# The first layer of an ELU network on one core: seven block products for the 384-token blocks too

## The chip, the core and the metric

The kernel runs on one core of one Trainium2 chip. The metric is the device time of one execution in microseconds (us). Before the change it is 615.97 us, the median of three runs (615.86 to 616.35). TensorE (PE) multiplies, with a row of its own for weight loads (PEld); VectorE (DVE) and ScalarE (ACT) work element by element, GpSimd (POOL) does one integer addition per weight tile, and SyncE (SP) issues nearly all transfers (DMAs).

## The reference

```python
# q, k, v: (4, 12, 448, 64); cap = 30
scores = cap * tanh(q @ k.T / sqrt(64) / cap)
attn = softmax(scores) @ v
x = attn.transpose(0, 2, 1, 3).reshape(1792, 768)     # tokens x d_model
h = x @ w_in                                           # 768 x 2048
g = where(h > 0, h, exp(min(h, 0)) - 1)
return g @ w_out                                       # 2048 x 768
```

## The kernel before, in words

First the attention (to about 161 us of the span), then the two-layer network, which the change is about. All matrices of the network stand transposed on the chip: 128 rows of d_model or d_ff by tokens. The 1792 tokens are four blocks t = 0 to 3, two of 384 tokens (the small blocks) and two of 512 (the large ones). d_model is six chunks of 128 (c), d_ff 16 tiles of 128, taken in eight rounds r = 0 to 7 of two tiles (`FT`). Every fp32 operand is split into a high and a low part, and a product is three matmuls: high by high, high by low, low by high (`products`, L404). So one chunk of the contraction costs three matmuls of one block's width.

A round has a first layer (`hidden`, L421: six chunks, 18 matmuls for each of two d_ff tiles and each block), the ELU (`exp` on ACT, `bend` on DVE, `high` on ACT, `low` on DVE) and a second layer (`pair`, L460: two output tiles e and e + 1, 12 matmuls together, in one of three rooms of two PSUM banks), whose result DVE adds to the sum over rounds (`gather`, L473).

From round 1 on the large blocks' first layer goes by seven products in place of eight. The pair of blocks by the two halves of d_model, and the two d_ff tiles by the same halves, are 2 by 2 quarters of three chunks each. Sums of x quarters and sums of weight quarters (`sum`, `form_high`, `form_low` of `Weights`, each round anew) are multiplied as blocks 1 to 7 (`block`, L483), nine matmuls each, m1 to m7. Blocks 6, 7, 4 and 5 take sums of x, which are formed once (`combine`, `form_high`, `form_low` of `Tokens`), stored in DRAM (`send`) and fetched every round into a ring of three buffers of one chunk (`fetch`, L288). m1 is copied out of PSUM by ACT (`keep`, c1), m6 is added to c1 (u2), m7 to u2 (u3), m4 to u3 (c), m2 to c1, m3 to u2, m5 to u3 and u2 (`add`, L495, on DVE). c, c1, u3 and u2 are then what `hidden` would have given, in SBUF and not in PSUM.

Blocks and `hidden` share two PSUM banks in turn (`bank`, L416): a block can't begin before the one two places ahead of it has been read out.

Each engine runs its instructions in program order. That order is written by a planner: a step has an engine, a duration, a due time, what it needs, and rooms it takes and frees; `Plan.run` plays the steps through and emits them in that order, the steps of TensorE in the order in which `plan_products` lists them. Weight tiles come through one raw buffer `pre` (`load`), then ACT, DVE and POOL unpack them (`plan_tile`) and DVE makes the weight sums (`plan_forms`). Transfers are steps of an engine d and stand in SP's queue in the order of the plan.

Of the kernel before, what the change touches and what calls it, by code (L numbers as in the profile page):

```python
# [213 lines left out]
class Tokens:  # L214


    def __init__(self, nc, pool, early):
# [32 lines left out]
    def first(self):  # L250
        for c in range(NC):
            self.parts[1, c] = [
                self.next.tile([P, BLOCKS[1][1]], F32R, name=f"x{i}1_{c}", tag=f"x{i}", bufs=NC) for i in "hl"
            ]

    def combine(self, i, k):

        x = [[self.block(HC * j + i, PAIR + n) for n in range(2)] for j in range(2)]
# [15 lines left out]
    def form_high(self, n, i):
        t = self.chunk(n, i)
        self.nc.scalar.activation(out=t[:, 0], in_=self.form(n, i), func=AF.Copy)
        self.ring.setdefault(n, []).append((t[:, 0], t[:, 1]))
        self.whole[n, i] = t

    def form_low(self, n, i):  # L280
        h, l = self.ring[n][i]
        self.nc.vector.tensor_tensor(out=l, in0=self.form(n, i), in1=h.bitcast(F32), op=ALU.subtract)

    def send(self, n, i):
        d = self.forms[n, i] = self.dr.tile([P, 2, BANK], F32, name=f"form{n}_{i}", tag=f"form{n}_{i}", bufs=1)
        self.nc.sync.dma_start(out=d, in_=self.whole.pop((n, i)).bitcast(F32))
# [981 lines left out]
```

## Time and profile before

| | |
|---|---|
| time, median of three runs | 615.97 us |
| time of the profiled execution | 616.79 us |
| its span, first to last instruction | 614.9 us |
| PE busy | 605.9 us, 99% |
| DVE busy | 475.9 us, 77% |
| ACT busy | 365.1 us, 59% |
| DMA, mean over the span | 168 GB/s, 49% of 16 engines |
| granted TensorE clock | 0.998 of full speed |

The 1.9 us between the span and the time lie outside the first and the last instruction. Matmuls overlap in the profile (a matmul of 384 columns is shown as 0.33 to 0.34 us long, while the next one starts about 0.17 us after it), so the pace is read from starts and not from durations. One round of the network is 55.7 us long, from 1 on; the last matmul starts at 608.5 us.

### The profile page before, as it was taken

The page shows a single profiled execution, that of the slowest core. Times are in us where ns is not written, and L with a number is a line of the kernel's source. Part 1 is how long each engine was busy: PE and PEld are TensorE (multiplying, and loading weights), DVE is VectorE, ACT ScalarE, POOL GpSimd, SP SyncE. Part 2 cuts the span into 40 slices and gives each one's busy share as a digit, 9 for nine tenths or more (in the row PEclk, how much of TensorE's full clock was granted, in tenths as well). Part 3 has the DMA queues.
Part 4 walks back from the last instruction along what each step waited for, and adds up shares of the span by engine and source line. Part 5 has one row for each costly group of instructions (what it writes and reads, how often), then busy time and mean ns, then how long its engine had stood idle before and what let it go on. Part 6 is the DMA issues. An engine that isn't in the chain of part 4 may idle for free.

```text
span 614.9 us, 8926 instructions
## 1 busy us (share of the span) xinstructions
PE 605.9 (99%) x3347; PEld 472.0 (77%) x3347; DVE 475.9 (77%) x684; ACT 365.1 (59%) x527; POOL 63.1 (10%) x40
## 2 busy tenths in 40 slices
PE   8999999999999999999999999999999999999996
PEld 3444444444788889888988988898899889888984
DVE  5898999998779966977896687779668857874473
ACT  6999999999876674724545354454445435441330
POOL 0010010010100112112102111211110112110000
PEclk9999999999999999999999999999999999999999
DMA  5456457571221778644535445464444445352444
GB/s 188 162 170 197 142 140 225 154 197 57 88 48 58 281 299 270 221 153 165 192 107 206 155 161 193 157 228 166 172 163 146 155 155 205 136 220 80 163 157 176
DMA packets 39622, 103.08 MB, mean 168 GB/s; under 512 B 11026, under 2 KB 15890, under 8 KB 39570
## 3 DMA queue, kind: packets, MB, share of 16 engines
q1 hardware_dynamic: 39282, 101.90, 48.9%
q8 instruction: 28, 0.46, 0.3%
q10 hardware_dynamic: 288, 0.52, 0.3%
q14 instruction: 24, 0.20, 0.1%
HBM read 90.44 MB, written 11.88 MB: 166 GB/s over the span
## 4 chain that ended last, share of the span: by engine, by line
PE 97%; ACT 1%; DMA 0%; DVE 0%; issue 0%; SPq 0%; ACTq 0%
PE o L408 12%; PE o L407 12%; PE o L406 12%; PE pv L861 10%; PE s L819 8%; PE h L407 6%; PE h L406 6%; PE h L408 6%; PE m L408 6%; PE m L407 6%; PE m L406 6%; PE sum L905 3%; PE pv L874 2%; PE s L836 2%; DMA pre<-in_qk_dram 0%; ACT p L854 0%
## 5 line engine op out<-in xcount | busy, mean ns | idle before, releaser
L408 PE MATMUL o<-gh,wl 128*128 128x384 f32 (+1 forms) x380 | 137.8, 363 | 0.0
L406 PE MATMUL o<-gh,wh 128*128 128x384 f32 (+1 forms) x380 | 137.6, 362 | 0.0
L407 PE MATMUL o<-gl,wh 128*128 128x384 f32 (+1 forms) x380 | 137.5, 362 | 0.0
L476 DVE TENSOR_TENSOR x<-o,x 128x768 f32<-128x768 f32 (+1 forms) x83 | 90.0, 1086 | 24.7 <-PE o L408 24.3
L148 POOL TENSOR_TENSOR wv<-wv,wq 128x768 int32<-128x768 int32 x24 | 46.7, 1946 | 370.0 <-DVE wv L145 354.6
L852 ACT ACTIVATE s<-s 128x896 f32<-128x896 f32 x84 | 76.6, 912 | 4.7 <-PE s L836 3.6
L854 ACT ACTIVATE p<-s 128x896 f32<-128x896 f32 x84 | 77.1, 918 | 2.7
L407 PEld LDWEIGHTS o<-gl,wh 128*128 128x128 f32 x380 | 71.4, 188 | 7.7
L408 PEld LDWEIGHTS o<-gh,wl 128*128 128x128 f32 x380 | 71.3, 188 | 7.7 <-DVE wl L159 0.2
L406 PEld LDWEIGHTS o<-gh,wh 128*128 128x128 f32 x380 | 71.4, 188 | 7.6
L407 PE MATMUL h<-xl,wh 128*128 128x384 f32 (+1 forms) x210 | 71.5, 340 | 0.0
L406 PE MATMUL h<-xh,wh 128*128 128x384 f32 (+1 forms) x210 | 71.5, 340 | 0.0
L408 PE MATMUL h<-xh,wl 128*128 128x384 f32 (+1 forms) x210 | 71.3, 339 | 0.0
L861 PE MATMUL pv<-p,vf 128*64 128x448 f32 x276 | 59.5, 552 | 0.0
L449 ACT ACTIVATE gh<-e 128x384 fp32r<-128x384 f32 (+1 forms) x64 | 36.7, 574 | 26.8 <-DVE e L439 26.6
L439 DVE SCALAR_TENSOR_TENSOR e<-e,h 128x384 f32<-128x384 f32 (+1 forms) x36 | 20.2, 564 | 33.1 <-ACT e L435 33.1
L453 DVE TENSOR_TENSOR gl<-e,gh 128x384 fp32r<-128x384 f32 (+1 forms) x64 | 40.0, 630 | 5.9 <-ACT gh L449 5.8
L406 PEld LDWEIGHTS h<-xh,wh 128*128 128x128 f32 x210 | 39.4, 188 | 3.0 <-DVE e L439 0.7
L407 PEld LDWEIGHTS h<-xl,wh 128*128 128x128 f32 x210 | 39.4, 188 | 2.1 <-DVE xl L248 0.8
L861 PEld LDWEIGHTS pv<-p,vf 128*64 128x64 f32 x276 | 16.8, 136 | 31.0 <-issue 23.3
L408 PEld LDWEIGHTS h<-xh,wl 128*128 128x128 f32 x210 | 39.4, 188 | 0.6
L434 ACT ACTIVATE e<-h 128x384 f32<-128x384 f32 (+1 forms) x36 | 18.0, 499 | 35.5 <-PE h L408 35.3
(132 smaller groups left out, 1019.2 us busy)
## 6 DMA issues: line engine op xcount, KB each, us to landing
t<-form SPq DMA_DIRECT2D x81, 512.0 KB, 5.5
pre<-in_w_dram SPq DMA_DIRECT2D x32, 768.0 KB, 4.4
raw<-in_qk_dram SPq DMA_DIRECT2D x22, 448.0 KB, 4.5
form<-t SPq DMA_DIRECT2D x12, 512.0 KB, 3.4
vf<-in_v_dram SPq DMA_DIRECT2D x23, 256.0 KB, 4.3
rb<-rec SPq DMA_DIRECT2D x48, 112.0 KB, 2.9
out_dram<-x SPq DMA_DIRECT2D x5, 512.0 KB, 2.8
out_dram<-x SPq DMA_DIRECT2D x6, 384.0 KB, 2.5
```

The source lines that it names most:

```text
L148: nc.gpsimd.tensor_tensor(out=vi, in0=vi, in1=q, op=ALU.add)
L406: mm(acc, wh[:, m, :], ph, start=first, stop=False)
L407: mm(acc, wh[:, m, :], pl, start=False, stop=False)
L408: mm(acc, wl[:, m, :], ph, start=False, stop=last)
L439: self.nc.vector.scalar_tensor_tensor(out=e, in0=e, scalar=-1.0, in1=self.h.pop(k), op0=ALU.add, op1=ALU.max)
L449: self.nc.scalar.activation(out=self.g[k][0], in_=self.e[k], func=AF.Copy)
L453: self.nc.vector.tensor_tensor(out=gl, in0=self.e.pop(k), in1=gh.bitcast(F32), op=ALU.subtract)
L476: self.nc.vector.tensor_tensor(out=o, in0=self.o.pop((r, t, e)), in1=o, op=ALU.add)
L819: yield lambda a=a, b=b, i=i: self.nc.tensor.matmul(s, a[o, k], b[o, :S], start=i == 0, stop=i == 2)
L852: self.nc.scalar.activation(out=s, in_=s, func=AF.Tanh, scale=self.con.tanh_scale)
L854: self.nc.scalar.activation(out=pt, in_=s, func=AF.Exp, scale=self.con.exp_scale)
L861: self.nc.tensor.matmul(out[o, :S], w[j], x[j], **flags)
```

## The change

The small blocks take the seven-product scheme too, from round 2 on (`FROM`); in rounds 0 and 1 they still go by `hidden`. `plan_block` has a second argument h: 1 for the large pair of blocks, 0 for the small. The names now carry it: m6_1_2 is block 6 of the large pair in round 2, m6_0_2 that of the small.

The small blocks' sums need x itself, while `leave` writes the second layer's sum over it; so the first 768 token columns of x are parked in DRAM (`park`, six transfers), taken back in twelve pieces (`unpark`), summed (`combine`, 12 on DVE), split (`form_high`, 12 on ACT, and `form_low`, 12 on DVE) through one of two buffers, and stored (`send`). Sums of both kinds are fetched every round. Three chunks of block 1's split x (c < 3 of t = 1) no longer stay in SBUF: round 1 fetches them (`plan_both`), which pays for two more buffers, "more", so that from round 2's small blocks on five buffers take the fetches in turn.

The order of TensorE's work is now a list for each kind of round (`ORDERS`): a number is a block (1 to 7 of the large pair, 11 to 17 of the small), a pair `(t, i)` a `hidden`, a triple `(back, t, e)` one output pair of the second layer of the round `back` rounds ago. Due times have changed too (`DUES`, `ELU`, `ADD`, `GATHER`, `LEAD`).

```diff
-NEXT = {6: (3, 0), 7: (4, 0), 4: (1, 0), 5: (2, 1)}
+ORDER = (*range(HC, NC), *range(HC))
+FROM = (2, 1)
+LEAD = 10.1
+DUES = ((-21.5, -17.4, -10.3, 4.0, 13.0), (-19.6, -29.7, -25.7, -5.8, 14.8), (-20.2, -16.9, -7.6, 6.0, 18.4))
...
+    (
+        6, 1, 2, 7, 3, (1, 3, 0), 4, (1, 3, 2), 11, (1, 3, 4), 5, (0, 2, 0), (0, 2, 2), (0, 2, 4), (0, 3, 0),
+        17, (0, 3, 2), (0, 3, 4), 16, 14, 12, 13, 15,
+    ),
...
+    def park(self, c):
+        width = 2 * BLOCKS[0][1]
+        d = self.kept[c] = self.dr.tile([P, width], F32, name=f"park{c}", tag=f"park{c}", bufs=1)
+        self.nc.sync.dma_start(out=d, in_=self.all[:, c, :width])
+
+    def unpark(self, j, k, i):
+        width = BLOCKS[0][1]
+        t = self.raw[j, k, i] = self.half.tile([P, width], F32, name=f"back{j}{k}{i}", tag="back", bufs=4)
+        self.nc.sync.dma_start(out=t, in_=self.kept[HC * j + i][:, k * width : k * width + width])
...
+    def fetch(self, h, r, n, i, room):
         if i == 0:
-            self.ring[n] = []
-        t = self.chunk(f"{r}_{n}", i)
-        self.nc.sync.dma_start(out=t.bitcast(F32), in_=self.forms[n, i])
-        self.ring[n].append((t[:, 0], t[:, 1]))
+            self.ring[h, n] = []
+        if room == "ring":
+            t = self.chunk(f"{h}_{r}_{n}_{i}")
+        else:
+            t = self.half.tile([P, 2, BANK], F32R, name=f"t{h}_{r}_{n}_{i}", tag="more", bufs=2)
+        t = t[:, :, : BLOCKS[2 * h][1]]
+        self.nc.sync.dma_start(out=t.bitcast(F32), in_=self.forms[h, n, i])
...
-    def plan_block(self, n, r):
+    def plan_block(self, n, h, r):
         p, x, wt = self.plan, self.x, self.wt
+        t, width = 2 * h, BLOCKS[2 * h][1]
...
+    def plan_fetches(self):
+
+        steps, turn = [], 0
+        for due, h, r, b, i in self.uses:
+            if (h, r, b) == (1, 1, 2):
+                continue
+            room = "ring"
+            if (r, h) >= (FROM[0], 0) and (r, h) != (FROM[0], 1):
+                room, turn = ("ring", "ring", "ring", "more", "more")[turn], (turn + 1) % 5
...
+        for r, order in enumerate(ORDERS[:3] + ORDERS[3:4] * (NR - 4) + ORDERS[4:]):
             self.begun[r] = self.clock
...
+            for k in order:
+                if isinstance(k, int):
+                    self.plan_block(k % 10, 1 - k // 10, r)
+                elif len(k) == 1:
+                    self.plan_both(r)
+                elif len(k) == 2:
+                    self.plan_first(r, *k)
+                else:
+                    back, t, e = k
+                    self.plan_second(r - back, t, e)
...
         p.room("ring", HC)
+        p.room("more", 2)
+        p.room("back", 4)
+        p.room("stage", 1)
+        p.room("wq", 1)
         self.plan_products()
+        self.plan_fetches()
         self.plan_opening(normalised)
+        self.plan_smaller(self.begun[FROM[0]])
```

Three places show how instructions move. The first is TensorE at the start of round 2. Before, block 1 (its last row stands here) is followed by block 6, and this by the small blocks' first layer (h4):

```order
L408 MATMUL m1_2_2889<-xh2_2_1945,wl8_2685 128x512
L406 MATMUL m6_2_2901<-t2_2_0_2811,forms_1889 128x512
L407 MATMUL m6_2_2901<-t2_2_0_2811,forms_1889 128x512
L408 MATMUL m6_2_2901<-t2_2_0_2811,forms_1889 128x512
L406 MATMUL m6_2_2901<-t2_2_1_2833,forms_1889 128x512
L407 MATMUL m6_2_2901<-t2_2_1_2833,forms_1889 128x512
L408 MATMUL m6_2_2901<-t2_2_1_2833,forms_1889 128x512
L406 MATMUL m6_2_2901<-t2_2_2_2840,forms_1889 128x512
L407 MATMUL m6_2_2901<-t2_2_2_2840,forms_1889 128x512
L408 MATMUL m6_2_2901<-t2_2_2_2840,forms_1889 128x512
L406 MATMUL h4_0_2919<-xh0_0_882,wh8_2684 128x384
```

Now block 6 comes first (its last row stands here), then block 1, and then block 2:

```order
L468 MATMUL m6_1_2_2969<-t1_2_2_2_2928,forms_1883 128x512
L466 MATMUL m1_1_2_2988<-xh2_0_1921,wh8_2785 128x512
L467 MATMUL m1_1_2_2988<-xl2_0_1922,wh8_2785 128x512
L468 MATMUL m1_1_2_2988<-xh2_0_1921,wl8_2786 128x512
L466 MATMUL m1_1_2_2988<-xh2_1_1941,wh8_2785 128x512
L467 MATMUL m1_1_2_2988<-xl2_1_1942,wh8_2785 128x512
L468 MATMUL m1_1_2_2988<-xh2_1_1941,wl8_2786 128x512
L466 MATMUL m1_1_2_2988<-xh2_2_1950,wh8_2785 128x512
L467 MATMUL m1_1_2_2988<-xl2_2_1951,wh8_2785 128x512
L468 MATMUL m1_1_2_2988<-xh2_2_1950,wl8_2786 128x512
L466 MATMUL m2_1_2_3019<-xh2_3_1974,wh8_2785 128x512
```

Block 2, the third in this order, takes the bank that block 6 had; before, the third there was h4, in the bank of block 1. Later in round 2, blocks 6 and 4 of the small pair stand next to each other, behind an output pair and ahead of blocks 2, 3 and 5:

```order
L468 MATMUL o2_3_4_3339<-gh5_3_3249,wl11_3173 128x512
L466 MATMUL m6_0_2_3357<-t0_2_2_0_3261,forms_1883 128x384
L467 MATMUL m6_0_2_3357<-t0_2_2_0_3261,forms_1883 128x384
L468 MATMUL m6_0_2_3357<-t0_2_2_0_3261,forms_1883 128x384
L466 MATMUL m6_0_2_3357<-t0_2_2_1_3279,forms_1883 128x384
L467 MATMUL m6_0_2_3357<-t0_2_2_1_3279,forms_1883 128x384
L468 MATMUL m6_0_2_3357<-t0_2_2_1_3279,forms_1883 128x384
L466 MATMUL m6_0_2_3357<-t0_2_2_2_3315,forms_1883 128x384
L467 MATMUL m6_0_2_3357<-t0_2_2_2_3315,forms_1883 128x384
L468 MATMUL m6_0_2_3357<-t0_2_2_2_3315,forms_1883 128x384
L466 MATMUL m4_0_2_3379<-t0_2_4_0_3331,wh9_2903 128x384
```

The bank of m4_0_2 is the one that block 7 (m7_0_2) had, two output pairs earlier.

The second place is VectorE ahead of the addition of block 6 in round 2. wv are weight tiles that are unpacked, wl and gl low parts, x_123 the sum over rounds, e the ELU. Before, the eleven instructions up to that addition are:

```order
L476 TENSOR_TENSOR x_123<-o1_1_4_2783,x_123 128x2x384
L439 SCALAR_TENSOR_TENSOR e3_3_2842<-e3_3_2842,u3_1_2631 128x512
L439 SCALAR_TENSOR_TENSOR e2_3_2860<-e2_3_2860,u2_1_2553 128x512
L476 TENSOR_TENSOR x_123<-o1_2_0_2818,x_123 128x2x512
L453 TENSOR_TENSOR gl3_3_2882<-e3_3_2842,gh3_3_2881 128x512
L453 TENSOR_TENSOR gl2_3_2886<-e2_3_2860,gh2_3_2885 128x512
L476 TENSOR_TENSOR x_123<-o1_2_2_2846,x_123 128x2x512
L129 TENSOR_SCALAR wv10_2797<-wv10_2797 128x768
L132 TENSOR_SCALAR wv10_2797<-wv10_2797 128x768
L145 SCALAR_TENSOR_TENSOR wv10_2797<-pre_73,wv10_2797 128x768
L501 TENSOR_TENSOR u2_2_2925<-c1_2_2905,m6_2_2901 128x512
```

Now the twelve up to it are these; stage is the low part of a small block's sum of x, and the lines that read pre_73 and wv9 into forms are weight sums:

```order
L338 TENSOR_TENSOR stage2_1_2948<-back111_2793,stage2_1_2948 128x384
L514 TENSOR_TENSOR gl3_3_2954<-e3_3_2897,gh3_3_2953 128x512
L241 TENSOR_TENSOR forms_1883<-pre_73,forms_1883 128x384
L241 TENSOR_TENSOR forms_1883<-wv9_2829,forms_1883 128x384
L241 TENSOR_TENSOR forms_1883<-pre_73,forms_1883 128x384
L241 TENSOR_TENSOR forms_1883<-wv9_2829,forms_1883 128x384
L159 TENSOR_SCALAR wv10_2925<-wv10_2925 128x768
L162 TENSOR_SCALAR wv10_2925<-wv10_2925 128x768
L175 SCALAR_TENSOR_TENSOR wv10_2925<-pre_73,wv10_2925 128x768
L500 SCALAR_TENSOR_TENSOR e2_3_2930<-e2_3_2930,u2_1_1_2567 128x512
L537 TENSOR_TENSOR x_123<-o1_2_0_2882,x_123 128x2x512
L562 TENSOR_TENSOR u2_1_2_3012<-c1_1_2_3006,m6_1_2_2969 128x512
```

From the addition of m4 in round 1 to this addition, the two included, VectorE had 34 instructions before. Now it has 36: 5 additions of a block, 4 sums of x (`combine`), 3 `form_low` of them, 8 instructions that unpack three weight tiles, 4 sums of weight quarters and their 4 low parts, 3 `bend`, 2 `low`, and 3 `gather` (two of 768 columns, one of 1024).

The third place is SP's queue in round 4. pre is a raw weight tile, t a fetched chunk of a sum of x. Before:

```order
L106 DMA pre_73<-in_w_dram 128x1536
L294 DMA t4_3_0_3882<-form3_0_2402 128x1024
L294 DMA t4_3_1_3897<-form3_1_2420 128x1024
L294 DMA t4_3_2_3913<-form3_2_2448 128x1024
L106 DMA pre_73<-in_w_dram 128x1536 x2
L294 DMA t4_4_0_4027<-form4_0_2302 128x1024
L294 DMA t4_4_1_4039<-form4_1_2357 128x1024
L294 DMA t4_4_2_4056<-form4_2_2375 128x1024
L106 DMA pre_73<-in_w_dram 128x1536
L294 DMA t4_1_0_4139<-form1_0_2261 128x1024
L294 DMA t4_1_1_4154<-form1_1_2310 128x1024
L294 DMA t4_1_2_4169<-form1_2_2361 128x1024
```

Now, a piece of the same round, with the small pair's blocks 7 (t0_4_3), 6 (t0_4_2) and 4 (t0_4_4):

```order
L354 DMA t0_4_3_0_4149<-form0_3_0_2690 128x2x384
L354 DMA t0_4_3_1_4160<-form0_3_1_2951 128x2x384
L136 DMA pre_73<-in_w_dram 128x1536
L354 DMA t0_4_3_2_4197<-form0_3_2_3181 128x2x384
L354 DMA t0_4_2_0_4217<-form0_2_0_2709 128x2x384
L354 DMA t0_4_2_1_4222<-form0_2_1_2963 128x2x384
L354 DMA t0_4_2_2_4249<-form0_2_2_3192 128x2x384
L354 DMA t0_4_4_0_4276<-form0_4_0_2810 128x2x384
L354 DMA t0_4_4_1_4282<-form0_4_1_3040 128x2x384
L354 DMA t0_4_4_2_4295<-form0_4_2_3227 128x2x384
```

In between, in both orders, stand the reads of other blocks' chunks that the pieces leave out. Twelve chunks a round were fetched; now it is 24 from round 2 on, between the same four weight tiles, and a fetch waits for the buffer of the fetch five places ahead of it.

## Rows read from the trace of the kernel before

**Rows 1.** The page's first part: busy us, share of the span, instructions.
```profile
PE 605.9 (99%) x3347; PEld 472.0 (77%) x3347; DVE 475.9 (77%) x684; ACT 365.1 (59%) x527; POOL 63.1 (10%) x40
```
**Rows 2.** Waits of PE behind its first instruction: us in total, times, longest.
```profile
PE s L836 <- DMA pre<-in_qk_dram: 0.8, 1, 0.8
PE s L819 <- ACT p L854: 0.7, 1, 0.7
```
**Rows 3.** Busy time of each engine in stretches of one round, 1 to 3.
```profile
core 0: us, PE busy (x) PEld busy (x) DVE busy (x) ACT busy (x) POOL busy (x), PEclk, DMA share, GB/s
208.20:263.90 55.70, 55.70 (x279) 49.97 (x278) 44.41 (x70) 36.94 (x59) 7.54 (x4) 1.00 0.72 257
263.90:319.60 55.70, 55.70 (x280) 50.13 (x279) 43.40 (x62) 25.46 (x41) 7.41 (x4) 1.00 0.49 170
319.60:375.30 55.70, 55.70 (x280) 50.13 (x279) 41.35 (x59) 25.39 (x41) 7.38 (x4) 1.00 0.49 170
```
**Rows 4.** Timeline of PE, round 2: start us, us, instruction; 17, 9, 36 matmuls between.
```profile
279.64 0.39 PE L407 MATMUL o<-gl,wh 128*128 128x512 f32 x1
...
283.49 0.40 PE L406 MATMUL m<-t,forms 128*128 128x512 f32 x1
...
285.59 0.33 PE L406 MATMUL h<-xh,wh 128*128 128x384 f32 x1
...
291.83 0.33 PE L406 MATMUL o<-gh,wh 128*128 128x384 f32 x1
```
**Rows 5.** Groups of VectorE instructions by form: busy us, mean ns, idle before.
```profile
L476 DVE TENSOR_TENSOR x<-o,x 128x1024 f32<-128x1024 f32 x41 | 50.0, 1221 | 17.0 <-PE o L408 16.9
L476 DVE TENSOR_TENSOR x<-o,x 128x768 f32<-128x768 f32 x42 | 40.0, 954 | 7.8 <-PE o L408 7.4
...
L145 DVE SCALAR_TENSOR_TENSOR wv<-pre,wv 128x768 int32<-128x768 int32 x24 | 22.9, 954 | 0.4
L159 DVE TENSOR_TENSOR wl<-wv,wh 128x768 fp32r<-128x768 f32 x24 | 22.9, 954 | 9.2 <-ACT wh L155 9.2
...
L453 DVE TENSOR_TENSOR gl<-e,gh 128x512 fp32r<-128x512 f32 x32 | 21.5, 682 | 0.7 <-ACT gh L449 0.7
...
L439 DVE SCALAR_TENSOR_TENSOR e<-e,h 128x384 f32<-128x384 f32 x32 | 17.6, 550 | 33.1 <-ACT e L435 33.1
...
L132 DVE TENSOR_SCALAR wv<-wv 128x768 int32<-128x768 int32 x24 | 13.4, 557 | 0.5
...
L211 DVE TENSOR_TENSOR forms<-pre,forms 128x384 fp32r<-128x384 f32 x14 | 7.7, 551 | 1.4 <-ACT forms L207 1.4
...
L201 DVE TENSOR_TENSOR pre<-pre 128x384 f32<-128x384 f32 x7 | 3.9, 558 | 0.2
```
**Rows 6.** Timeline at round 2's blocks 1 and 6: their last matmuls, copy, addition.
```profile
266.72 0.39 PE L408 MATMUL m<-xh,wl 128*128 128x512 f32 x1
...
267.15 0.60 ACT L493 ACTIVATE c<-m 128x512 f32<-128x512 f32 x1 [3.48 <-PE m L408]
...
268.82 0.39 PE L408 MATMUL m<-t,forms 128*128 128x512 f32 x1
...
269.32 0.69 DVE L501 TENSOR_TENSOR u<-c,m 128x512 f32<-128x512 f32 x1 [0.80 <-PE m L408]
```
**Rows 7.** Line L294, the fetches: from issue to landing, over 81 fetches.
```profile
DMA to landing us min/median/max: 3.4/5.5/8.3
```
**Rows 8.** Line L439, `bend`: duration ns min/median/max, from PSUM, from SBUF.
```profile
L439 DVE SCALAR_TENSOR_TENSOR e<-e,h x36: 486/554/681, 160.7 to 572.9; 128x384 f32<-128x384 f32 x32, 128x512 f32<-128x512 f32 x4
...
L439 DVE SCALAR_TENSOR_TENSOR e<-e,u x14: 678/683/2243, 261.7 to 596.5; 128x512 f32<-128x512 f32 x14
```
**Rows 9.** DMA in round 1's stretch, 208.2 to 263.9 us: GB/s in 40 slices.
```profile
GB/s 403 412 394 18 338 394 394 179 362 303 294 150 371 124 341 365 315 204 287 172 354 303 318 150 309 229 332 291 300 165 71 247 265 9 59 335 382 324 35 0
```

More of the change, by code (lines that the diff above doesn't have):

```diff
@@ L250, in first @@
     def first(self):
[L251 to L258, printed above, removed]
+        width = BLOCKS[1][1]
+        for c in range(HC, NC):
+            self.parts[1, c] = [self.next.tile([P, width], F32R, name=f"x{i}1_{c}", tag=f"x{i}", bufs=HC) for i in "hl"]
@@ new lines, in second, with part, change @@
+    def second(self):
+        self.half = self.open("half")
+        for c in range(HC):
+            t = self.whole[0, 0, c] = self.half.tile([P, 2, BLOCKS[1][1]], F32R, name=f"x1_{c}", tag="x1", bufs=HC)
+            self.parts[1, c] = [t[:, 0], t[:, 1]]
+    def part(self, r, t, c):
+        return self.ring[0, 0][c] if r and t == 1 and c < HC else self.parts[t, c]
+    def change(self, name):
+        self.shut("half")
+        self.half = self.open(name)
+    def park(self, c):
+        width = 2 * BLOCKS[0][1]
+        d = self.kept[c] = self.dr.tile([P, width], F32, name=f"park{c}", tag=f"park{c}", bufs=1)
+        self.nc.sync.dma_start(out=d, in_=self.all[:, c, :width])
@@ L264, in combine, with chunk, form @@
         )[k]
+        o, a, b = (self.raw[*n, i] if small else self.block(HC * n[0] + i, PAIR + n[1]) for n in (o, a, b))
         self.nc.vector.tensor_tensor(out=o, in0=a, in1=b, op=ALU.subtract)
-    def chunk(self, n, i):
-        return self.back.tile([P, 2, BANK], F32R, name=f"t{n}_{i}", tag="ring", bufs=HC)
-    def form(self, n, i):
+    def chunk(self, n):
+        return self.back.tile([P, 2, BANK], F32R, name=f"t{n}", tag="ring", bufs=HC)
+    def form(self, h, n, i):
         j, k = {1: (0, 0), 3: (0, 1), 2: (1, 1), 4: (1, 0)}[n]
-        return self.block(HC * j + i, PAIR + k)
@@ L274, in form_high @@
[L274 to L286, printed above, removed]
@@ L288, in fetch, with form_high @@
-    def fetch(self, r, n, i):
-        if r >= NR:
-            return
-        if i == 0:
-            self.ring[n] = []
-        t = self.chunk(f"{r}_{n}", i)
-        self.nc.sync.dma_start(out=t.bitcast(F32), in_=self.forms[n, i])
-        self.ring[n].append((t[:, 0], t[:, 1]))
-    def quarter(self, j, k):
-        return [self.parts[PAIR + k, HC * j + i] for i in range(HC)]
+        return self.block(HC * j + i, PAIR + k) if h else self.raw[j, k, i]
+    def form_high(self, h, n, i, other=False):
+        if h:
+            t = self.chunk(f"{n}_{i}")
+            self.ring.setdefault((h, n), []).append((t[:, 0], t[:, 1]))
+        else:
+            pool, tag = (self.weights.pool, "wq") if other else (self.half, "stage")
+            t = pool.tile([P, 2, BLOCKS[0][1]], F32R, name=f"stage{n}_{i}", tag=tag, bufs=1)
+        self.whole[h, n, i] = t
+        self.nc.scalar.activation(out=t[:, 0], in_=self.form(h, n, i), func=AF.Copy)
@@ L301, with quarter @@
+    def quarter(self, h, j, k):
+        return [self.parts[2 * h + k, HC * j + i] for i in range(HC)]
 class Step:
@@ L528, in plan_first @@
         bank = ("h", r, t, i)
-        for c in range(NC):
-            more = {"takes": ("bank", bank)} if c == 0 and (r, t) != (0, 0) else {}
+        for k, c in enumerate(ORDER if t == 1 else range(NC)):
+            more = {"takes": ("bank", bank)} if k == 0 and (r, t) != (0, 0) else {}
             needs = [("w", self.tile(f, 0))] + [("x", t, c)] * (t > 0)
-            if c == NC - 1:
+            if k == NC - 1:
                 more["gives"] = ("p", r, t, i)
@@ L541, in plan_second @@
         needs = [("g", r, t, i) for i in range(FT)] + [("w", self.tile(r * FT + i, 1)) for i in range(FT)]
-        for e in range(0, NC, 2):
+        for e in range(0, NC, 2) if only is None else (only,):
             single = last and e == NC - 2
@@ L652, in plan_tile, with users @@
+    def users(self, r, i):
+        keys = []
+        for h in range(2):
+            if r < FROM[h]:
+                keys += [("p", r, 2 * h + j, i) for j in range(2)]
+            else:
+                keys += [("m", n, h, r) for n in ((1, 2), (4,))[i]]
+        return keys
     def plan_tile(self, k, due):
```

284 lines of the change are left out of this document (178 added, 106 removed), and 3 rows, old and new, of the table ORDERS.

## The prediction

> **What bounds the kernel now.** I read the busy shares first: TensorE (PE) is busy 99% of the span, VectorE (DVE) 77%, ScalarE 59% [rows 1]. Busy can hide waiting, so the waits of PE come next: behind its first instruction no wait is longer than 0.8 us [rows 2]. The stretches of one round then say the same of the part that changes: PE 55.70 of 55.70 us, DVE 41 to 44 us, the DMA engines about half busy, but 0.72 in round 1 [rows 3]. So the time of the network is the number of matmuls by their pace, and whatever takes matmuls away helps as long as PE still never waits.
>
> The pace comes from starts [rows 4]. 36 matmuls of 384 columns on x in SBUF take 291.83 - 285.59 = 6.24 us, 0.1733 us each. 17 of the second layer's 512 columns take 3.85 us, 0.2265 each; 9 of 512 columns on a fetched chunk take 2.10 us, 0.2333 each. The granted clock is 1.00 throughout [rows 3].
>
> **What goes.** In rounds 2 to 7 the small pair has 7 blocks of 9 matmuls in place of 4 `hidden` of 18: 63 for 72, so 54 matmuls of 384 columns less. 54 x 0.1733 = 9.4 us off the path, if nothing else moved.
>
> **What comes, beside other work.**
>
> - DVE gains, in each round from 2 on, seven additions of 384 columns out of PSUM. None stands in the trace; the nearest is the `bend` of 384 columns, which reads PSUM and SBUF too, 0.550 us [rows 5]. 7 x 0.55 = 3.9 us on a round of 41 to 43 [rows 3]: 45 to 47 of a round that is now 55.7 - 1.6 = 54.1 us. It fits, and PE hides it. ScalarE gains one copy a round and has the room (25 us of 55.7).
> - Once, 12 `combine` and 12 `form_low` of 384 columns, the first of them in round 1 and the last in round 2. Like weight sums (0.558) and their low parts (0.551) [rows 5]: 24 x 0.55 = 13.2 us. DVE in rounds 1 and 2 then has 44.4 + 43.4 + 13.2 + 3.9 = 104.9 us in 55.7 + 54.1 = 109.8 us. That is 96%; here PE is no longer a safe cover.
> - SP gains 75 fetches of 0.39 MB (12 a round from 2 on, 3 in round 1). A later round moves 170 GB/s x 55.7 us = 9.5 MB [rows 3], plus 12 x 0.39 = 14.2 MB in 54.1 us, 262 GB/s. Round 1 of before ran at 257 GB/s and PE did not wait there [rows 2, 3], so the later rounds are covered on the mean. Rounds 1 and 2 move 14.3 + 9.5 MB of before, 15 fetches (5.9), 12 stores of small sums (4.7) and 8 `unpark` of 0.2 (1.6): 36 MB in 109.8 us, 328 GB/s. The single slices of round 1 go to 412 [rows 9]. So it fits, with little to spare.
>
> **What comes on the path.** Three waits of PE, all in rounds 1 and 2, and a slower pace.
>
> 1. *Block 2 of the large pair in round 2.* It needs block 6's bank, so the addition of m6 must be over, and this stands behind 35 other DVE instructions, counted from the addition of m4 in round 1. Their sum [rows 5, 6, 8]: 5 additions at 0.69, 3 `bend` at 0.683, 4 `combine` and 3 `form_low` at 0.551, 2 long unpacking ones and 2 low parts of weight tiles at 0.954, 4 short unpacking ones at 0.557, 4 weight sums at 0.558 and 4 low parts at 0.551, 2 low parts of 512 at 0.682, and gathers of 0.954, 0.954 and 1.221. That is 3.45 + 2.05 + 3.86 + 3.82 + 2.23 + 2.23 + 2.20 + 1.36 + 3.13 = 24.3 us. DVE can't begin it before block 4's last matmul plus the 0.50 us between 268.82 and 269.32 [rows 6], so m2 starts 24.8 us after that matmul at the earliest. PE alone would be there after 0.23 + block 3 (9 x 0.2265 = 2.04) + two output pairs of 384 (24 x 0.1733 = 4.16) + block 5 (2.10) + three pairs of 512 (36 x 0.2265 = 8.15) + blocks 6 (2.10) and 1 (2.04) = 20.8 us. PE waits 4.0 us somewhere on this way, block 5's fetch and block 6's weight sums included: whichever is late first, DVE sets the end. Before, 34 instructions of much the same sum lay from the one addition to the other, but PE had block 2 and a third pair of 384 more there (4.1 us), and so 0.80 us of idle time still stood ahead of the last addition [rows 6]. If some of this DVE work overlapped less badly than counted, the floor is the chain in itself: block 1's last matmul, copy by ScalarE (starts 0.43 us later, takes 0.60), addition 0.69: 1.72 - 0.23 = 1.5 us.
> 2. *Block 4 of the small pair in round 2* follows block 6 at once and needs block 7's bank; m7 can be added only to u2, which the addition of m6 makes. 0.50 + 0.55 + 0.55 us after block 6's last matmul, less the 0.17 at which PE would go on: 1.4 us. From round 3 on an output pair (12 matmuls of 512, 2.7 us) or more stands between, and hides it.
> 3. *The third chunk of a block in round 2*, three fetches behind stores and a weight tile. A fetch lands after 3.4 to 8.3 us, 5.5 the median [rows 7]. One chunk late by 0 to 5.5 - 3.4 = 2.1 us; I take 0.4, near zero, since round 1 of before had the same load and no wait.
> 4. *The pace on fetched chunks.* 216 matmuls (4 blocks x 9 x 6 rounds) that read fetched chunks of 384 columns do not stand in the trace. Between 0.1733 and 0.1733 + (0.2333 - 0.2265) = 0.180 us: 0 to 1.5 us in sum; I take half, 0.8.
>
> The waits come to 4.0 + 1.4 + 0.4 + 0.8 = 6.6 us, and the change to -9.4 + 6.6 = -2.8 us. The profiled execution took 616.79 us (614.9 of span and 1.9 around it), so 614.0 by its measure; the median of the runs is 0.8 lower, 615.97 - 2.8 = 613.2 us.
>
> **Rivals.**
>
> *The gain comes through.* DVE's work in the first wait may be lighter than the means make it, and only the two short chains are left: -9.4 + 1.5 + 1.4 = -6.5, 609.5 us. For it: nearly all of that work comes in forms that are in the trace, and a little could be done before block 4. Against: they stand in that order in the program, and no engine overtakes itself.
>
> *A fetch is late in each of the later rounds (slower).* In round 4 the third chunk of block 6 of the small pair gets the buffer of block 7's first chunk. From there to its use PE has two more chunks (6 x 0.1733 = 1.04 us), an output pair of 512 (12 x 0.2265 = 2.72) and two chunks of block 6 (1.04): 4.8 us. A fetch that lands in the median 5.5 us costs 0.7 a round, in 7 us 2.2, in 8.3 us 3.5. Rounds 3 to 6 have this order. At 7 us, 4 x 2.2 = 8.8: 622.0 us; the gain is undone from 0.7 us a round, which is the median. For it: that median. Against: the 3.4 us are a fetch alone, the longer ones had two or three issued at once [rows 7], and this one is alone in SP's queue. The Trainium skill (DMA: Bandwidth & Descriptors, "Where 436 GB/s comes from") says that about 358 GB/s bind between HBM and SBUF; the slices above 358 in round 1 do not agree with it as a hard limit here [rows 9]. By it rounds 1 and 2 would be 328 / 358 = 92% full, and by the highest slice 80%: the first would give this rival twice the chance that the second does.
>
> *VectorE is held up by GpSimd in the later rounds (slower).* In rounds 2 to 7 four `bend` a round go from PSUM and SBUF to two inputs in SBUF. Of this kind one took 2.24 us in place of 0.683; none that reads PSUM was over 0.681 [rows 8]. The small pair's blocks 2, 3 and 4 stand behind each other in rounds 2 to 6, and each bank has 9 x 0.1733 = 1.56 us to come back, of which 0.50 + 0.55 - 0.17 = 0.9 are taken by the addition: 0.7 us of slack. One hold-up of 1.56 us at that place costs 0.9 us, 4.5 us in five rounds: 617.7 us. It undoes the gain from three such hits. For it is the rule in the Trainium skill (SBUF — State Buffer, "Who interferes with whom") that a VectorE instruction with two SBUF inputs contends with a GpSimd one that reads SBUF, and one of the two then blocks fully; the 2.24 us agree. Against: one in 14 was hit, and GpSimd works only 7.4 us of a round [rows 3].
>
> **How the numbers follow.** 0.64 for the forecast, with a range of its own from 611.5 (the third and fourth term zero, half a us less in the first) to 616 (the third and fourth at their upper ends, DVE 1 us late at the start of the first). 0.10 for the full gain, 0.12 for late fetches, 0.14 for GpSimd. The range 610 to 619 leaves out less than two in ten: half of the first rival below, most of the late fetches above. What a measurement of this kernel can tell from no change is about 0.2%, 1.2 us, so faster means under 614.7. The forecast is under it with about 0.8 of its chance (0.51), within it with 0.16 of 0.64 (0.10): faster 0.51 + 0.10 = 0.61; same 0.10 and 0.05 of the two slow rivals in their mild forms, 0.15; slower 0.24.
>
> **What would show it.** Right: 54 matmuls fewer; PE starts 4 us apart in sum between block 5 of round 1 and block 2 of round 2, 1.4 us ahead of the small pair's block 4 in round 2, and none from round 3 on; a later round about 54 us long, with DVE at 46 and the DMA near 262 GB/s; 0.174 to 0.180 us a matmul in the small blocks on fetched chunks. Wrong: gaps of PE that return every round, at a fetched chunk (the second rival) or with a VectorE instruction over 2 us ahead of them (the third); a wait in round 2 under 2 us (the first); or a wait before round 1, where I count none.

## The result and the profile after

The changed kernel takes 625.09 us (median of four runs, 622.63 to 626.76), the kernel before 615.91 beside it: a ratio of 1.0145, 95% interval 1.0108 to 1.0182. It is slower by 9 us, where 2.8 us less were forecast. The profiled execution took 624.2 us and spans 622.4.

The first part of the page (answers to [rows 1]):

```profile
PE 603.7 (97%) x3293; PEld 464.5 (75%) x3293; DVE 516.8 (83%) x750; ACT 370.3 (59%) x545; POOL 64.5 (10%) x40
```

54 matmuls fewer, as counted, but PE no longer fills its span. Its waits from 165 us on (answer to [rows 2]; us in total, times, longest):

```profile
PE m L466 <- DMA t<-form: 4.5, 7, 1.4
PE m L466 <- DVE u L562: 3.1, 2, 1.8
PE h L467 <- DVE xl L278: 2.8, 2, 2.0
```

The windows (columns as in [rows 3]) say where. The first row is the opening of the network, then the end of round 1, the start of round 2, round 3, and a later round:

```profile
165.00:185.00 20.00, 17.22 (x86) 15.45 (x85) 12.91 (x25) 13.55 (x25) 0.00 (x0) 0.90 0.82 251
...
255.00:275.00 20.00, 17.93 (x80) 14.00 (x79) 18.54 (x28) 11.34 (x20) 2.15 (x1) 1.00 0.85 300
275.00:295.00 20.00, 17.85 (x77) 13.87 (x76) 18.54 (x29) 7.96 (x13) 3.32 (x2) 1.00 0.92 329
...
325.00:380.00 55.00, 53.59 (x270) 48.07 (x270) 44.94 (x67) 27.35 (x46) 7.58 (x4) 1.00 0.86 299
380.00:435.00 55.00, 55.00 (x274) 49.26 (x273) 47.69 (x68) 25.16 (x42) 7.58 (x4) 1.00 0.76 260
```

The later round is as forecast: PE full, DVE 47.7 of 55 us, 260 GB/s; round 4 is 54.5 us long (block 1 starts at 384.94 us there and at 439.44 in round 5). The opening is not as forecast. The same stretch of the kernel before:

```profile
165.00:185.00 20.00, 20.00 (x105) 18.02 (x104) 14.82 (x26) 13.96 (x25) 1.50 (x1) 1.00 0.20 52
```

The DMA share went from 0.20 to 0.82 there, and PE lost 2.8 us and a tenth of its clock. SP's queue shows what was added. Before (start us, us, what, how many):

```profile
161.57 0.52 SPq L106 DMA_DIRECT2D pre<-in_w_dram  x1
162.53 2.39 SPq L920 DMA_DIRECT2D den<-sums  x4
168.09 0.63 SPq L928 DMA_DIRECT2D rec<-den  x1
169.03 6.20 SPq L936 DMA_DIRECT2D rb<-rec  x6
```

After:

```profile
161.33 0.58 SPq L301 DMA_DIRECT2D park<-x  x1
162.55 2.42 SPq L1056 DMA_DIRECT2D den<-sums  x4
165.01 2.56 SPq L301 DMA_DIRECT2D park<-x  x4
167.74 0.84 SPq L1064 DMA_DIRECT2D rec<-den  x1
168.62 0.97 SPq L301 DMA_DIRECT2D park<-x  x1
169.63 1.12 SPq L1072 DMA_DIRECT2D rb<-rec  x2
170.86 0.55 SPq L136 DMA_DIRECT2D pre<-in_w_dram  x1
171.76 1.08 SPq L1072 DMA_DIRECT2D rb<-rec  x2
```

The chain den, rec, rb ends the attention: `rb` carries the reciprocal sums with which DVE normalises the last parts of x. Six parks now stand among it, and the weight tile `pre` (0.79 MB), which the planner's transfer engine could no longer fit ahead of them, has moved from 161.57 to 170.86 us, in front of the second `rb`. The first `rb` lands after 5.3 to 5.4 us, the second after 6.2 to 7.0 (before: 2.7 to 3.7). DVE then stands:

```profile
169.86 0.55 DVE L500 SCALAR_TENSOR_TENSOR e<-e,h 128x384 f32<-128x384 f32 x1
175.67 0.63 DVE L1077 TENSOR_TENSOR x<-num,rb 128x448 f32<-128x448 f32 x1 [5.26 <-DMA rb<-rec]
...
179.25 0.63 DVE L1077 TENSOR_TENSOR x<-num,rb 128x448 f32<-128x448 f32 x1 [1.42 <-DMA rb<-rec]
179.80 0.68 DVE L278 TENSOR_TENSOR xl<-x,xh 128x512 fp32r<-128x512 f32 x1
```

The split `xl` of block t = 2 stands behind these normalisations, and PE waits for it. What follows on PE, and then the windows of two stretches of it (the third number from the end is the granted clock):

```profile
178.10 0.39 PE L466 MATMUL h<-xh,wh 128*128 128x512 f32 x1
180.53 0.50 PE L467 MATMUL h<-xl,wh 128*128 128x512 f32 x1 [2.04 <-DVE xl L278]
...
182.58 0.79 PE L467 MATMUL h<-xl,wh 128*128 128x512 f32 x1 [0.74 <-DVE xl L278]
183.17 0.63 PE L468 MATMUL h<-xh,wl 128*128 128x512 f32 x1
183.59 0.63 PE L466 MATMUL h<-xh,wh 128*128 128x512 f32 x1
```

```profile
180.50:182.50 2.00, 1.30 (x3) 0.54 (x3) 1.67 (x4) 2.00 (x5) 0.00 (x0) 0.62 0.64 256
182.50:187.40 4.90, 4.82 (x11) 3.80 (x12) 4.90 (x10) 0.41 (x1) 0.00 (x0) 0.50 0.54 161
```

From 183.17 to 187.43 us the starts lie 0.427 us apart, not 0.227: the granted clock is 0.50, the lower of the two levels (1.2 of 2.4 GHz). It fell at 181.0 us, between the two waits, and rose at 187.8. Starts above the pace add up to 6.1 us in the opening, some 3.6 of waiting and 2.5 of clock, against 0.5 before.

### The profile page after: what moved, and what is told of

The parts are those of the page before. It is cut to its first block, busy times and chain, and to the rows that moved or that the text cites. A ratio compares the mean times of both kernels' runs of the same rounds, so it can differ in the third digit from the quotient of the medians.

```text
span 622.4 us, 9163 instructions
## 1 busy us (share of the span) xinstructions
PE 603.7 (97%) x3293; PEld 464.5 (75%) x3293; DVE 516.8 (83%) x750; ACT 370.3 (59%) x545; POOL 64.5 (10%) x40
## 4 chain that ended last, share of the span: by engine, by line
PE 87%; DMA 7%; DVE 3%; ACT 1%; issue 1%; SPq 0%; DVEq 0%; ACTq 0%
PE o L467 11%; PE o L468 11%; PE o L466 11%; PE pv L997 10%; PE s L955 8%; PE m L466 8%; PE m L467 8%; PE m L468 8%; DMA t<-form 4%; PE sum L1041 3%; PE h L467 2%; PE h L468 2%; PE pv L1010 2%; PE h L466 2%; DMA rb<-rec 1%; PE s L972 1%
## 5 line engine op out<-in xcount | busy, mean ns | idle before, releaser
L178 POOL TENSOR_TENSOR wv<-wv,wq 128x768 int32<-128x768 int32 x24 | 48.1, 2004 | 354.6 <-DVE wv L175 346.5
L185 ACT ACTIVATE wh<-wv 128x768 fp32r<-128x768 f32 x22 | 18.5, 841 | 49.4 <-POOL wv L178 49.3
L510 ACT ACTIVATE gh<-e 128x384 fp32r<-128x384 f32 (+1 forms) x64 | 34.9, 570 | 20.7 <-DVE e L500 15.6
L466 PE MATMUL m<-t,forms 128*128 128x512 f32 (+1 forms) x117 | 43.5, 371 | 3.4 <-DMA t<-form 3.3
L148 ACT ACTIVATE wv<-pre 128x768 f32<-128x768 f32 x22 | 19.8, 900 | 40.7 <-DMA pre<-in_w_dram 40.7
L468 PE MATMUL m<-t,forms 128*128 128x512 f32 (+1 forms) x117 | 43.2, 369 | 0.0
L467 PE MATMUL m<-t,forms 128*128 128x512 f32 (+1 forms) x117 | 43.1, 368 | 0.0
L514 DVE TENSOR_TENSOR gl<-e,gh 128x384 fp32r<-128x384 f32 (+1 forms) x64 | 38.4, 626 | 5.5 <-ACT gh L510 5.3
L997 PEld LDWEIGHTS pv<-p,vf 128*64 128x64 f32 x276 | 16.8, 136 | 31.0 <-issue 23.5
L562 DVE TENSOR_TENSOR u<-u,m 128x512 f32<-128x512 f32 (+1 forms) x52 | 31.5, 624 | 9.9 <-PE m L468 9.4
L496 ACT ACTIVATE e<-e 128x384 f32<-128x384 f32 (+1 forms) x64 | 37.1, 580 | 2.0
L495 ACT ACTIVATE e<-c 128x512 f32<-128x512 f32 (+1 forms) x26 | 15.2, 584 | 38.0 <-DVE c L562 38.0
```

What stands on the lines that cost most here:

```text
L178: nc.gpsimd.tensor_tensor(out=vi, in0=vi, in1=q, op=ALU.add)
L466: mm(acc, wh[:, m, :], ph, start=first, stop=False)
L467: mm(acc, wh[:, m, :], pl, start=False, stop=False)
L468: mm(acc, wl[:, m, :], ph, start=False, stop=last)
L496: self.nc.scalar.activation(out=e, in_=e, func=AF.Exp, scale=-1.0)
L510: self.nc.scalar.activation(out=self.g[k][0], in_=self.e[k], func=AF.Copy)
```

## The experiments

Each time is the median of four runs (ten for e2), with the lowest and the highest; a ratio is to the kernel before, which took 616.0 to 616.2 us beside them. "Excess" is the sum of PE's start-to-start times above the pace (0.2265 us for 512 columns, 0.1735 for 384). The diffs show the lines that matter.

**The opening: parks issued during the attention** (e1_parks_early; 619.59 us, 617.71 to 623.45; ratio 1.0045, 1.0027 to 1.0062).

```diff
-        p.thread(*(Step("d", 1.25, 2.0 * c, x.park, c, gives=("parked", c)) for c in range(NC)))
...
+            at(58.0 + 2.5 * c, self.x.park, c)
```

> The changed kernel with its six park transfers issued one by one during the attention (about 110 to 135 us), none behind 145 us. Theory A (in the opening the parks, 2.36 MB, stand in SP's queue ahead of the transfers den, rec and rb of the attention's last pairs; VectorE then stands 5.3 and 1.4 us at a normalisation, the split of block t = 2 comes late, PE waits 2.2 and 1.1 us and runs at the half clock until 187.8): the opening's excess over the pace falls from 5.8 to about 0.5 us, the time of a profile like the one of after (624.2) to 619, the median from 625.1 to 618.5-620, still slower than before. Theory C (the stall comes from the x1 stores and buffers that are also new there): 624 to 626, no change.

Theory A: 5.5 us come back and the opening's excess is 0.3 us. Its profiled run is the slowest of the four, with 0.9 us of waiting in the attention (`PE sum` for `DVE u`); two loads of q and k issued behind a park landed after 8.5 and 9.2 us.

**The parks alone, in the kernel before** (e2_before_parks; 617.10 us; ratio 1.0014, 1.0005 to 1.0024).

```diff
+        p.thread(*(Step("d", 1.25, 2.0 * c, x.park, c, gives=("parked", c)) for c in range(NC)))
```

> The kernel before with the six park transfers alone added in the opening, at the due times that the changed kernel has; nothing reads what they store. Theory A: they cost what the opening cost, 4 to 6 us, half of it by the clock: 620 to 622. Theory C: 616 to 617.

A miss: 1.0 us, not 4 to 6. There the planner put the weight tile at 166.69 us, ahead of `rec`, and the excess is 1.6 us.

**The parks on ScalarE's queue** (e3_parks_on_act; 625.59 us, 624.78 to 625.81).

```diff
-        self.nc.sync.dma_start(out=d, in_=self.all[:, c, :width])
+        self.nc.scalar.dma_start(out=d, in_=self.all[:, c, :width])
```

> The changed kernel with the six park transfers issued by ScalarE's queue at the same places of the plan, so that in SP's queue nothing stands behind them; the bytes in the opening are the same. If the order in SP's queue is what delays the small transfers (A1): the opening's excess is 0.5 to 1.5 us and the time 619 to 621. If it is the load on the DMA engines, whichever queue it comes from (A2): rb still lands late, excess 4 to 6 us, 624 to 626.

The landings and the time go A2's way: the two pairs of `rb` still take 5.0 to 6.4 us. But the opening's excess is 3.2 us, between the two theories: PE waits 2.6 us in place of 2.8, and the clock doesn't fall there. It falls at 278.5 and 333.1 us instead, behind waits that after has too, and 1.7 us of waits stand between 205 and 250 us that after hasn't. Nor is SP's queue free of large transfers: the weight tile is issued at 170.69 us, between the two pairs of `rb`, as in after. So this run doesn't settle whether the queue or the load delays them. The Trainium skill (DMA: Bandwidth & Descriptors, "Queues, rings and completion order") says that a DMA engine serves the queues in turn, packet by packet. By that the first pair, which had no large transfer ahead of it in its own queue, should have come through sooner; it took 5.0 to 5.5 us in place of 5.3 to 5.4, with the weight tile 0.6 to 1.5 us behind it.

**The weight tile back ahead of the parks** (e8_weights_first; 620.64 us, 620.29 to 620.94; ratio 1.0075, 1.0058 to 1.0091).

```diff
-            Step("d", 2.4, due - 11.0, wt.load, needs=(("raw", k - 1),)),
+            Step("d", 2.4, due - 11.0 - 50.0 * (k == 4), wt.load, needs=(("raw", k - 1),)),
```

> The changed kernel with its parks where they are, and only the weight tile of 0.79 MB moved back ahead of them in SP's queue (in before it was issued at 161.57 us, in after at 170.86, between the transfers rb of two normalisations, and the second rb then took 6.2 to 7.0 us). If the moved weight tile makes the difference between the 1.0 us of e2_before_parks and the 5.3 us of after: the opening's excess falls to 1 to 2.5 us, 621 to 622.5. If the parks and the x1 stores alone make it: 624 to 626.

One transfer moved in one queue gives 4.4 us back, more than expected. The first pair of `rb` lands after 3.6 to 3.7 us, the second after 4.8 to 5.0, and PE waits 1.4 us in place of 2.8:

```profile
PE h L467 <- DVE xl L278: 1.4, 2, 0.9
```

The clock stays at the upper level (0.996 to 0.998 over the runs), and the opening's excess is 1.9 us. So the parks cost 1.0 to 1.4 us (e2's time, e8's excess less the 0.5 of before), and the weight tile that they pushed between two pairs of `rb` most of the rest.

**Parks spread, none ahead of a load** (e5_parks_spread; 620.42 us, 618.87 to 620.92).

```diff
+PARKS = (50.0, 54.4, 61.4, 75.31, 75.4, 77.5)
...
+            at(PARKS[c], self.x.park, c)
```

> As e1_parks_early, but each park stands behind the loads of q, k and v of its round in SP's queue, none ahead of one (in e1's profile two loads behind parks landed after 8.5 and 9.2 us and the attention ended 1.6 us later). If the parks themselves were e1's cost: attention as long as before (last sum at 160 us and not 161.6), 617.5 to 619. If not: 619.6 as e1.

No gain over e1, though the attention's last sum begins 1.7 us sooner in the profile: the two scatter by more. It is the base of what follows but for e4.

**No VectorE work for the small sums** (e4_no_small_dve; 635.52 us, 634.10 to 636.43).

```diff
-                    Step("v", dve(width), at + k, x.combine, i, k, True, needs=[("raw", *o, i) for o in order[k:][:2]],
+                    Step(None, 0.0, at + k, None, needs=[("raw", *o, i) for o in order[k:][:2]],
...
-                Step("v", dve(width), at + 0.6, x.form_low, 0, n, i, frees=(("back", *o, i),), gives=("turn", k)),
+                Step("s", act(width), at + 0.6, x.form_low, 0, n, i, frees=(("back", *o, i),), gives=("turn", k)),
```

> The changed kernel with early parks (as in e1_parks_early), and of the small blocks' sums VectorE has nothing: the 12 combines are left out and the low halves are plain copies by ScalarE (so the sums are not the sums). Transfers are the same in number and size. Theory D (in rounds 1 and 2 VectorE's chain of 36 instructions sets when large block 2 of round 2 starts; 11 of the 36 are these sums, 6 us): PE's excess between block 5 of round 1 and block 2 of round 2 falls from 5.6 to at most 2 us, and the time is 3.5 to 4.5 us under e1_parks_early, about 615. Rival F (the fetched chunks are late by themselves, from SP's order and the load): the 2.7 us at block 5 of round 1 and the 0.8 at block 6 of round 2 remain, and only the wait at block 2 goes: 2 us under e1_parks_early, about 617.

Neither theory; the time is 16 us over e1's. ScalarE had 12 more copies, and PE waited 3.0 us for its `wh` at 236 us; the clock fell behind three waits (at 240.5, 281.4 and 339.4 us). Block 2 still began 1.99 us late. VectorE's chain up to it had 30 instructions, none of them for the sums, but took 23.5 us, 3.4 of which VectorE waited for PE.

**Round 2: block 1 ahead of block 6** (e6_block1_first; 620.02 us, 619.31 to 623.16).

```diff
-        6, 1, 2, 7, 3, (1, 3, 0), 4, (1, 3, 2), 11, (1, 3, 4), 5, (0, 2, 0), (0, 2, 2), (0, 2, 4), (0, 3, 0),
+        1, 6, 2, 7, 3, (1, 3, 0), 4, (1, 3, 2), 11, (1, 3, 4), 5, (0, 2, 0), (0, 2, 2), (0, 2, 4), (0, 3, 0),
```

> As e5, and in round 2 the large pair's block 1 stands ahead of block 6 and not behind it. Theory D of the prediction (VectorE's long chain of 36 instructions sets when m6 is added): the 2.0 us ahead of block 2 come back ahead of block 7, which now waits for that addition: 0 to 0.5 us under e5. Theory S (only the short chain block 1, copy, addition sets it, the 1.72 us of the prediction's floor, since the same 1.98 to 1.99 us stood there in four profiles, in e4 without 11 of the 36 instructions): 2.0 us under e5.

Theory D: the wait doesn't go, it moves to block 7 and grows, with 40 instructions and 27.4 us in the chain (245 to 290 us):

```profile
PE m L467 <- DVE u L563: 2.7, 1, 2.7
PE m L467 <- DMA t<-form: 1.8, 5, 0.8
```

**The same with the additions first on VectorE** (e9_additions_first; 620.91 us, 619.50 to 623.30).

```diff
-        due = end + ADD
+        due = end + ADD - 14.0 * ((h, r) == (1, 2))
```

> As e6 (block 1 ahead of block 6 in round 2), and the additions of round 2's large blocks get a due time 14 us earlier, so that VectorE does them ahead of the gathers and unpacking that wait beside them. In e6 block 7 waited 2.8 us for the addition of m6, which stood behind 16 us of other VectorE work without a gap. If only the place in VectorE's queue matters: this wait goes and nothing takes its place, 2.5 us under e6, about 617.5. If the fetches are as late as VectorE (in e6 block 7's third chunk landed at 279.8 us, 1.3 us after block 7 began): block 7 now waits 1 to 2 us for a chunk, and the gain is 0.5 to 1.5 us.

The second case, without its gain. VectorE's wait is gone from this stretch, and the waits for fetched chunks have doubled:

```profile
PE m L467 <- DMA t<-form: 3.6, 5, 1.4
```

The clock falls behind them (0.50 from 279.9 to 283.3 us).

**e6 with both pairs behind blocks 17 and 16** (e7_pairs_between; 623.59 us, 622.15 to 624.83).

```diff
-        17, (0, 3, 2), (0, 3, 4), 16, 14, 12, 13, 15,
+        17, 16, (0, 3, 2), (0, 3, 4), 14, 12, 13, 15,
```

> As e6, and at the end of round 2 the two output pairs stand between the small pair's blocks 17, 16 and its 14, 12, 13, 15, in place of between 17 and 16. The wait of 1.42 us for the addition of m6 and m7 should go (an output pair of 2.7 us covers the 1.65 us chain). Theory L (fetched chunks are late because twelve of them are used within 15 us there): the wait of 1.2 to 1.8 us at block 6 of round 3 stays, since block 4's and 5's fetches are as close as before; in sum 1.4 to 2 us under e6. If the chunks of block 16 now come late, the gain is eaten.

The 1.42 us ahead of block 14 went; 1.9 us at block 16's third chunk came, so the gain was eaten, and 1.4 remained in round 3. Block 7's wait grew to 3.6 us, and the clock fell behind it.

**One pair each** (e10_one_pair_each; 622.16 us, 620.47 to 624.00).

```diff
-        17, (0, 3, 2), (0, 3, 4), 16, 14, 12, 13, 15,
+        17, (0, 3, 2), 16, (0, 3, 4), 14, 12, 13, 15,
```

> As e5, and at the end of round 2 one output pair stands between blocks 17 and 16 and one between 16 and 14. The pair of 2.7 us covers the chain of copy and additions, so the 1.42 us ahead of block 14 go. If the fetches have room: 1.5 us under e5 or a little more (618.5 to 619). If block 16's chunks are late because one pair less stands ahead of them: 0 to 0.5 us under e5.

Not faster than its base. From 305 to 345 us the base had

```profile
PE m L467 <- DMA t<-form: 1.4, 1, 1.4
PE m L467 <- DVE u L563: 1.3, 1, 1.3
```

and this one

```profile
PE o L467 <- ACT gh L511: 1.5, 1, 1.5
PE o L468 <- DVE gl L515: 0.4, 1, 0.4
PE m L467 <- DMA t<-form: 0.3, 1, 0.3
```

Of the two old waits 0.3 us is left, and the first output pair of round 3 now waits for the ELU of the blocks just before it, which the old waits had hidden. The clock falls there (0.50 from 330.7 to 334.1 us), which it didn't in the base.

**Sums not formed** (e11_sums_not_formed; 623.85 us, 622.49 to 624.82).

```diff
+                p.known["stored", 0, n, i] = 0.0
...
-        self.nc.sync.dma_start(out=t.bitcast(F32), in_=self.forms[h, n, i])
+        form = self.forms[h, n, i] if (h, n, i) in self.forms else self.forms[1, n, i][:, :, : BLOCKS[0][1]]
+        self.nc.sync.dma_start(out=t.bitcast(F32), in_=form)
```

> As e5, but the small blocks' sums are not formed: no unparking (2.4 MB), no combine, split or store (4.7 MB, 24 VectorE and 12 ScalarE instructions); their fetches take 384 columns of the large blocks' sums, the same count and bytes on chip. What is left is the steady state of the new scheme. If the forming makes the waits of rounds 1 and 2: of e5's 6 us there at most 1.5 remain, and the time is 615 to 616. If the added fetches alone make them: within 1.5 us of e5.

A miss of both theories. The fetches' waits there fall from 1.6 to 0.9 us, but PE waits 3.5 us at block 2 in place of 1.7 (245 to 290 us), and its clock falls behind that (0.91 in 275 to 295 us):

```profile
PE m L468 <- DVE u L564: 3.5, 1, 3.5
PE m L468 <- DMA t<-form: 0.9, 3, 0.4
```

Between block 5's last addition and the one of m6 VectorE worked 10.3 us without a gap, and none of it belongs to the sums: unpacking, `bend`, gathers, low parts. One `bend` took 2.3 us, over an addition of GpSimd (267.19 to 269.32 us).

**All orders and due times chosen anew** (e12_new_order; 625.14 us, 623.45 to 626.31). Of eight lists, the one of round 2:

```diff
+        1, 6, (1, 2, 2), 2, 7, 3, 11, (1, 3, 0), 4, (1, 3, 2), (1, 3, 4), 5, (0, 2, 2), (0, 2, 4), (0, 2, 0), 17,
+        (0, 3, 0), 16, (0, 3, 4), 14, 13, 12, 15,
```

> As e5, with the order of TensorE's work and the due times of all rounds chosen anew (in round 2: 1, 6, an output pair, then 2; 17, pair, 16, pair, 14, 13, 12, 15; in the later rounds pairs between most blocks). Both chains of copy and addition are covered by pairs and the fetches lie further apart: 3 to 5 us under e5, 615 to 617, level with the kernel before. If the load of rounds 1 and 2 is the limit in whatever order: 0 to 2 us under e5.

A miss. The wait at block 2 is gone and the end of round 2 has about 1 us left, but PE waits 1.8 us in the opening, its clock falls there and at 263 us, and round 6 has waits of 2.2 and 1.4 us for VectorE that were not there. So much changes at once here that the run doesn't test the load of rounds 1 and 2 by itself. No version tried beats the kernel before.

## Why the prediction was wrong

| step | predicted, us | measured |
|---|---|---|
| 54 matmuls of 384 columns | -9.4 | -9.4 |
| opening, ahead of round 1 | 0 | +5.6 |
| block 5 of round 1 to block 2 of round 2 | +4.0 | +5.5 |
| third chunks in round 2 | +0.4 | +1.3 |
| small block 4 in round 2 | +1.4 | +1.6 |
| pace on fetched chunks | +0.8 | +0.3 |
| fetches in rounds 3 and 7 | 0 | +2.4 |
| sum | -2.8 | +7.3 |

The column on the right is read from the profiled runs: the last matmul starts 7.8 us later than before, and the run takes 7.4 us more. The other three runs lie up to 2.6 us higher or 1.6 lower, with a mean clock of 0.989, 0.991 and 0.997 against 0.994; they have no trace, so where their clock fell is not shown.

**The step that failed is the opening**, "a wait before round 1, where I count none". It measured +5.6 us, and e1 and e8 give 5.5 and 4.4 us of it back. The transfers were counted for rounds 1 and 2 alone: fetches, stores, unparks. The six parks and the place of the weight tile in SP's queue were in the program's order, at a chain whose length PE's slack just covered. With +5.6 in place of 0 the forecast would have been 618.8, slower. The fetches add 3.3 us to what was forecast and the long chain 1.5. Freed of the opening's loss the kernel is still slower, 619.6 in e1: 1.9 us of new waits stand between 205 and 235 us there (a `leave` and two fetches; in after PE came later and none stood), and the next two points remain.

**The long chain was the right limit; that its length came so near is in part luck.** From the addition of m4 to the end of that of m6 24.3 us were forecast. The rows of after, VectorE and then GpSimd:

```profile
254.12 0.69 DVE L562 TENSOR_TENSOR c<-u,m 128x512 f32<-128x512 f32 x1
254.72 0.55 DVE L317 TENSOR_TENSOR back<-back,back 128x384 f32<-128x384 f32 x1
...
262.06 2.19 DVE L338 TENSOR_TENSOR stage<-back,stage 128x384 fp32r<-128x384 f32 x1
...
279.26 0.68 DVE L562 TENSOR_TENSOR u<-c,m 128x512 f32<-128x512 f32 x1
```

```profile
261.69 2.15 POOL L178 TENSOR_TENSOR wv<-wv,wq 128x768 int32<-128x768 int32 x1 [9.68 <-DVE wv L175]
```

It took 25.8 us (279.94 - 254.12). The low part at 262.06 us took 2.19 and not 0.55, over the rest of GpSimd's addition. The third rival's rule, the Trainium skill's on interference (SBUF — State Buffer, "Who interferes with whom"), agrees with this, in a place where the prediction did not look for it. No run moves GpSimd's addition away, so the cause is read from the overlap alone. The same hold-up, 2.16 to 2.18 us, stands in the chain of the five variants that kept this order (e1, e3, e5, e8, e10); their chains are 24.3 to 24.9 us and their excess 4.0 to 4.6 us. Each excess is the chain less 20.3 us (PE's own way of 20.8, less the 0.5 by which VectorE begins later) to within 0.1, as is after's 25.8 - 20.3 = 5.5. Which of PE's waits comes first on the way changes; the sum does not.

The luck is in the sum of durations. In the rows an instruction begins before the one ahead of it ends (254.12 + 0.69 is 254.81, the next begins at 254.72), so 24.3 counts 1.7 us of after's chain twice. Against it stand the hold-up (1.6 us) and 1.5 us in which VectorE did nothing; the forecast had neither. In the five variants the three nearly cancel.

Where the third rival did look for its hold-ups, in the later rounds, they came and cost nothing (`bend` on values in SBUF, 310 to 600 us; duration ns min/median/max, as in [rows 8]):

```profile
L500 DVE SCALAR_TENSOR_TENSOR e<-e,c x22: 548/682/2198, 327.6 to 597.0; 128x384 f32<-128x384 f32 x12, 128x512 f32<-128x512 f32 x10
```

Three of them took 2.20 us, at 374.41, 428.89 and 537.92 us (rounds 3, 4 and 6), each over an addition of GpSimd. By the prediction three hits at its place undo the gain; these fell elsewhere, and PE waits for nothing from 345 to 545 us.

VectorE's load alone does not set the chain's length. Without the sums' instructions it was 24.1 us (e11), since VectorE then waited 2.6 us in it, for PE and for ScalarE. With the additions put first (e9) the wait went to the fetches. That order, fetches and load are all near their limit fits these runs; none of them separates the three.

**The second rival came true in part**: no wait in rounds 4 to 6, but 1.3 us in round 3 and 1.15 in round 7. Round 2 has two late third chunks, 0.7 us each, at large block 4 and at its last block, 15. The waits at 15 and in round 3 stand where blocks 16, 14, 15 and round 3's 6 use twelve chunks within some 15 us. The landings (answer to [rows 7]; KB, median us):

```profile
t<-form SPq DMA_DIRECT2D x81, 512.0 KB, 5.7
t<-form SPq DMA_DIRECT2D x75, 384.0 KB, 4.6
```

The median hardly moved from 5.5. That points to the burst and not to the mean load; no run shows it by itself.

**Durations held.** The additions of 384 columns, the combines and the low parts (answers to [rows 5]):

```profile
L562 DVE TENSOR_TENSOR u<-u,m 128x384 f32<-128x384 f32 x24 | 12.7, 552 | 4.8 <-PE m L468 4.5
...
L338 DVE TENSOR_TENSOR stage<-back,stage 128x384 fp32r<-128x384 f32 x12 | 9.9, 827 | 1.1 <-ACT stage L334 1.1
L317 DVE TENSOR_TENSOR back<-back,back 128x384 f32<-128x384 f32 x12 | 6.7, 555 | 0.4 <-DMA back<-park 0.3
```

0.55 us was right for the first and the last; 0.827 for the split is 0.55 and two hold-ups among the twelve (2.20 us at 234.18 and 2.19 at 262.06), both over an addition of GpSimd. The matmuls on fetched chunks of 384 columns start 0.1748 us apart, those of `hidden` before 0.1734: 216 times 0.0014 is the 0.3 of the table.

One sum of the prediction is off: the upper end of the forecast's own range, by the terms that it names, is 613.2 + 1.7 + 0.7 + 1 = 616.6 and not 616. The measured time is far above either.

## What to carry to other kernels

Count a new scheme's one-off transfers in the stretch where they are issued, with everything that they push back in the queue; ask there which small transfer ends a chain. A transfer that only moves by 9 us can cost more than six that are added (here 4.4 us against 1.0 to 1.4). A sum of durations is not the length of a chain: it counts overlaps twice and leaves out hold-ups and gaps, and the errors can hide each other. Where order, fetches and an engine's load are all near their limit, removing one wait only shows the next.
